# A two-block transformer kernel: the softmax-free attention's reciprocal moved from VectorE to ScalarE as Ln and Exp, and layernorm, transposes and loads issued earlier

## The chip, the cores and the metric

One core of one Trainium2 chip. The time is the device time of the kernel in microseconds; lower is better. Engines are called PE (TensorE), DVE (VectorE), ACT (ScalarE), POOL (GpSimd) and SP (which here only issues DMA). L165 is line 165 of the kernel that the profile belongs to. psum is the memory to which PE writes its products; they share a few buffers there (four of them tagged "mm"), each in use until ACT or DVE has read it.

## The reference

Two block types alternate, A B A B, on a bf16 tensor of 2048 tokens by 1024 features. A is linear attention, B a bilinear gated MLP without activation.

```python
def _A_ref(x, wqkv, wo):            # 32 heads of 32
    q, k, v = split(x @ wqkv)
    phi = lambda t: jnp.where(t > 0, t + 1, jnp.exp(t)) + 1e-6
    pq, pk = phi(q), phi(k)
    kv  = einsum("bhsd,bhse->bhde", pk, v);  z = einsum("bhsd->bhd", pk)
    num = einsum("bhqd,bhde->bhqe", pq, kv)
    den = einsum("bhqd,bhd->bhq", pq, z)[..., None] + 1e-6
    return (num / den) @ wo
def _B_ref(x, w_gate, w_up, w_down):
    return ((x @ w_gate) * (x @ w_up)) @ w_down
x = x + _A_ref(_layernorm(x), ...);  x = x + _B_ref(_layernorm(x), ...)   # and both once more
```

## The kernel before

Tokens are handled in four groups of 512 (four tiles of 128). The order of instructions on each engine is chosen by a scheduler when the kernel is built (the *compiled order*); the program gives it priorities and data dependences. An A layer has two stages. The *projection stage* makes phi(q), phi(k), v and adds up the key-value sums. The *output stage* is what this study is about:

```python
def layer_A():
    with tc.tile_pool(name="pA", bufs=1) as pA:
        pqT = pA.tile([P, KD, S], BF16, tag="pqT")
        KVm = pA.tile([P, KD, 2, P], BF16, tag="KVm")
        with ...:                                  # projection stage
            # ... wqkv loaded, per group: ln_transpose x4, q, k, v, key-value products (cut)
        with tc.tile_pool(name="pA2", bufs=1) as p2, tc.tile_pool(name="wA2", bufs=2) as work:
            # ... wo loaded here (cut)
            for g in range(NG):                    # output stage
                oT = work.tile([P, KD, G], BF16, tag="oT")
                for c in range(KD):
                    nps = psum.tile([P, NB], F32, tag="mm", bufs=4)      # numerator
                    nc.tensor.matmul(out=nps[:], lhsT=KVm[:, c, 0, :], rhs=pqT[:, c, g * G:(g + 1) * G], ...)
                    dps = psum.tile([P, NB], F32, tag="mm", bufs=4)      # denominator
                    nc.tensor.matmul(out=dps[:], lhsT=KVm[:, c, 1, :], rhs=pqT[:, c, g * G:(g + 1) * G], ...)
                    den = work.tile([P, NB], F32, tag="den")
                    nc.scalar.activation(out=den[:], in_=dps[:], func=ACT.Identity, bias=eps6[:], scale=1.0)
                    nc.vector.reciprocal(out=den[:], in_=den[:])
                    nc.vector.tensor_tensor(out=oT[:, c, :], in0=nps[:], in1=den[:], op=ALU.mult)
                for tl in range(TPG):              # output projection, 64 products per group
                    # ... ps = oT @ wo ; X += ps on DVE (cut)
```

`ln_transpose` (bn_stats, Sqrt on ACT, normalise on DVE, eight transposes on PE, a copy on ACT) stands at the head of each group, in A and in B. In B the gate and up weights stream through two buffers each, and each group ends with 224 down products.

## Time and profile before

The median is 1940.78 us (6 runs, 1938.94 to 1944.26). I cut the timeline at four kinds of marks on PE: the first projection product, the last key-value product, the first gate product, the last down product.

| stretch | layer 1 and 2, us | layer 3 and 4, us |
|---|---|---|
| start to first projection product | 18.1 | 5.7 (from the last down product) |
| projection stage | 202.5 | 197.3 |
| output stage (to first gate product) | 165.0 | 164.8 |
| gated layer | 591.4 | 590.9 |
| end | | 3.6 |

The page of the kernel before: busy time by engine, then forty equal slices of the span, each digit a tenth of busy share; PEclk is the granted PE clock in tenths.

```profile
PE 1765.8 (91%) x8320; PEld 805.7 (42%) x8320; DVE 889.6 (46%) x1287; ACT 359.7 (19%) x567; POOL 166.6 (9%) x138
...
PE   7999666799999999999999995677999999999999
...
DVE  8877899931131131121277769999211111111111
...
PEclk9999877899999999999999997788999999999999
```

PE is busy 91% of the span, and at full clock nearly everywhere; the two dips (slices 5 to 8 and 25 to 28, PE at 5 to 7, PEclk at 7 to 8) are the two output stages, and there DVE stands at 9. The table of stretches for just these two gives, per engine, busy microseconds and the number of instructions (POOL last), then PEclk:

```profile
core 0: us, PE busy (x) PEld busy (x) DVE busy (x) ACT busy (x) POOL busy (x), PEclk, DMA share, GB/s
220.60:385.60 165.00, 101.78 (x360) 38.18 (x361) 160.05 (x153) 28.97 (x44) 0.00 (x0) 0.74 0.13 40
1179.90:1344.70 164.80, 100.46 (x361) 37.74 (x361) 159.98 (x153) 28.97 (x44) 0.00 (x0) 0.76 0.13 40
```

DVE is busy 160 of 165 us. PE counts 101 us of work, but the 320 products of the stage (256 projections, 64 numerators and denominators) would take 69 us at the spacing seen where PE is never interrupted (224 down products in 48.35 us, 0.216 us each). So the stage is DVE bound, and PE work in it also runs slowly. The groups by line, with count, then busy us and mean ns of one, then the idle time before them and its releaser (what ended the wait), name the culprit:

```profile
L165 DVE RECIPROCAL den<-den 128x512 f32<-128x512 f32 x64 | 211.3, 3327 | 3.4 <-ACT den L164 3.4
...
L164 ACT ACTIVATE den<-dps,eps 128x512 f32<-128x512 f32 x64 | 43.7, 686 | 242.9 <-DVE oT L166 207.8 <-PE dps L161 18.2 <-DVE KVm L147 16.8
...
L74 ACT ACT_TABLE_LOAD x12 | 15.4, 1283 | 10.0 <-DMA X<-in_A_x_dram 9.8
L87 ACT ACT_TABLE_LOAD x11 | 14.1, 1283 | 0.2
```

One reciprocal of 128x512 takes 3327 ns, nearly five times any other DVE pass over that shape here (at most 0.69 us). ACT_TABLE_LOAD, 1283 ns each, is the instruction that the build puts on ACT before a function of another set. The timeline (start, duration, engine, line, what, and in brackets the idle time before it with its releaser) shows how it holds PE:

```profile
231.87 1.22 DVE L166 TENSOR_TENSOR oT<-nps,den 128x512 bf16<-128x512 f32 x2
232.55 0.59 PE L158 MATMUL nps<-pqT,KVm 128*128 128x512 bf16 x1 [5.98 <-DVE oT L166]
...
232.59 0.69 ACT L164 ACTIVATE den<-dps,eps 128x512 f32<-128x512 f32 x1 [6.66 <-DVE oT L166]
...
233.31 6.56 DVE L165 RECIPROCAL den<-den 128x512 f32<-128x512 f32 x2 [0.22 <-ACT den L164]
...
240.48 0.59 PE L158 MATMUL nps<-pqT,KVm 128*128 128x512 bf16 x1 [3.50 <-DVE oT L166]
```

Two reciprocals (6.56 us), two products, and only then a psum buffer for the next numerator: PE waits 5.98 us. The matmul after that wait takes 0.59 us instead of 0.38, and after the next such waits products follow 0.43 us apart instead of 0.216: PE restarted at a lower clock. The totals of the waits of PE say the same (us in total, times, longest); the third line is the transposes, which wait for ACT to empty a psum buffer:

```profile
PE nps L158 <- DVE oT L166: 63.0, 12, 6.0
PE ps L172 <- DVE oT L166: 35.0, 8, 4.5
...
PE pt L81 <- ACT xnT L82: 9.2, 17, 0.7
```

### The profile page before, as it was taken

What the parts mean: (1) busy time and instruction counts of PE and PEld (TensorE: products, weight loads), DVE (VectorE), ACT (ScalarE), POOL (GpSimd) and SP (SyncE); (2) the same over time, 40 slices, a digit from 0 to 9 for tenths busy, and PEclk for the clock granted to TensorE, in tenths of its full rate; (3) what the DMA queues carried; (4) which work ended last, traced back from release to release, by engine and by line L of the source; (5) the groups of instructions that cost most, each with busy time, mean ns of one, the idle gap of its engine ahead of it and who ended that gap; (6) DMA issues with size and microseconds to landing.
All of it is one profiled execution on the core that took longest, in us unless ns stands there. A gap on an engine that the chain in (4) does not pass through costs nothing.

```text
span 1939.3 us, 19949 instructions
## 1 busy us (share of the span) xinstructions
PE 1765.8 (91%) x8320; PEld 805.7 (42%) x8320; DVE 889.6 (46%) x1287; ACT 359.7 (19%) x567; POOL 166.6 (9%) x138
## 2 busy tenths in 40 slices
PE   7999666799999999999999995677999999999999
PEld 3444322344444444444444442223444444444444
DVE  8877899931131131121277769999211111111111
ACT  4332111111021021021043321112211111110110
POOL 3344100000000000000034341000000000000000
PEclk9999877899999999999999997788999999999999
DMA  6000400074044134124040004002740440450420
GB/s 217 1 1 1 130 0 0 20 263 145 29 128 133 44 106 155 44 87 130 1 131 1 1 1 130 0 0 81 243 132 22 151 153 22 131 173 23 130 87 22
DMA packets 145882, 158.57 MB, mean 82 GB/s; under 512 B 3456, under 2 KB 134528, under 8 KB 145792
## 3 DMA queue, kind: packets, MB, share of 16 engines
q1 hardware_dynamic: 135424, 138.42, 22.3%
q10 hardware_dynamic: 10368, 18.88, 2.8%
q8 instruction: 65, 1.06, 0.2%
q14 instruction: 25, 0.20, 0.0%
HBM read 153.09 MB, written 4.19 MB: 81 GB/s over the span
## 4 chain that ended last, share of the span: by engine, by line
PE 79%; DVE 13%; issue 3%; ACT 2%; DMA 1%; POOL 0%; ACTq 0%; DVEq 0%; POOLq 0%
PE ps L216 20%; PE gp L202 20%; PE up L206 20%; PE ps L124 11%; DVE den L165 8%; PE ps L114 5%; PE ps L172 3%; ACT xnT L82 2%; DVE oT L166 1%; DVE X L175 1%; PE kp L138 1%; DVE acc L143 1%; DMA wd<-in_B_w_down_dram 1%; DMA X<-in_A_x_dram 1%; DVE st L70 0%
## 5 line engine op out<-in xcount | busy, mean ns | idle before, releaser
L210 DVE TENSOR_TENSOR hT<-gs,up 128x512 bf16<-128x512 f32 x224 | 153.8, 687 | 599.7 <-PE up L206 575.9
L202 PE MATMUL gp<-xnT,wg 128*128 128x512 bf16 x1792 | 423.3, 379 | 4.6 <-ACT xnT L82 4.3
L206 PE MATMUL up<-xnT,wu 128*128 128x512 bf16 x1792 | 423.3, 379 | 0.0
L216 PE MATMUL ps<-wd,hT 128*128 128x512 bf16 x1792 | 388.1, 379 | 0.0
L202 PEld LDWEIGHTS <-wg 128*128 128x128 bf16 x1792 | 175.3, 98 | 215.3 <-issue 5.8
L206 PEld LDWEIGHTS <-wu 128*128 128x128 bf16 x1792 | 175.4, 98 | 211.4
L216 PEld LDWEIGHTS <-hT 128*128 128x128 bf16 x1792 | 175.4, 98 | 211.4
L209 ACT COPY gs<-gp 128x512 f32<-128x512 f32 x224 | 130.9, 585 | 626.2 <-PE gp L202 608.6
L124 PE MATMUL ps<-wqkv,xnT 128*128 128x512 bf16 x1024 | 234.0, 379 | 0.0
L165 DVE RECIPROCAL den<-den 128x512 f32<-128x512 f32 x64 | 211.3, 3327 | 3.4 <-ACT den L164 3.4
L172 PE MATMUL ps<-wo,oT 128*128 128x512 bf16 x512 | 152.3, 449 | 52.3 <-DVE oT L166 35.0
L219 DVE TENSOR_TENSOR X<-X,ps 128x512 bf16<-128x512 bf16 x64 | 44.0, 687 | 338.5 <-PE ps L216 338.5
L124 PEld LDWEIGHTS <-xnT 128*128 128x128 bf16 x1024 | 100.1, 98 | 105.5
L82 ACT COPY xnT<-pt 128x1024 bf16<-128x1024 bf16 x64 | 61.2, 1019 | 374.2 <-PE pt L81 374.1
L87 ACT ACTIVATE m<-m 128x512 f32<-128x512 f32 x128 | 80.1, 630 | 235.7 <-DVE m L86 235.5
L114 PE MATMUL ps<-xnT,wqkv 128*128 128x512 bf16 x512 | 119.4, 397 | 4.6 <-ACT xnT L82 4.1
L172 PEld LDWEIGHTS <-oT 128*128 128x128 bf16 x512 | 55.1, 109 | 151.5 <-issue 66.8
L86 DVE TENSOR_SCALAR m<-ps 128x512 f32<-128x512 f32 x128 | 88.1, 688 | 47.2 <-PE ps L114 34.3
L158 PE MATMUL nps<-pqT,KVm 128*128 128x512 bf16 x64 | 32.8, 512 | 70.6 <-DVE oT L166 63.0
L90 POOL TENSOR_TENSOR pk<-m,r 128x512 bf16<-128x512 f32 x64 | 81.0, 1267 | 130.4 <-ACT m L87 127.7
L90 POOL TENSOR_TENSOR pqT<-m,r 128x512 bf16<-128x512 f32 x64 | 81.1, 1272 | 119.9 <-ACT m L87 85.7
L164 ACT ACTIVATE den<-dps,eps 128x512 f32<-128x512 f32 x64 | 43.7, 686 | 242.9 <-DVE oT L166 207.8
(33 smaller groups left out, 727.8 us busy)
## 6 DMA issues: line engine op xcount, KB each, us to landing
wg<-in_B_w_gate_dram SPq DMA_DIRECT2D x56, 1024.0 KB, 5.4
wu<-in_B_w_up_dram SPq DMA_DIRECT2D x56, 1024.0 KB, 7.2
wd<-in_B_w_down_dram ACTq DMA_DIRECT2D x56, 256.0 KB, 4.7
wqkv<-in_A_wqkv_dram SPq DMA_DIRECT2D x12, 1024.0 KB, 11.8
wo<-in_A_wo_dram SPq DMA_DIRECT2D x4, 1024.0 KB, 9.4
X<-in_A_x_dram ACTq DMA_DIRECT2D x8, 256.0 KB, 5.8
X<-in_A_x_dram SPq DMA_DIRECT2D x8, 256.0 KB, 5.6
out_dram<-X SPq DMA_DIRECT2D x8, 256.0 KB, 2.0
```

Of the source, the lines that this page charges most:

```text
L82: nc.scalar.copy(out=xnT[:, :, col0:col0 + P], in_=pt[:])
L86: nc.vector.tensor_scalar_min(out=m[:], in0=ps, scalar1=0.0)
L90: nc.gpsimd.tensor_tensor(out=dst, in0=m[:], in1=r[:], op=ALU.add)
L114: nc.tensor.matmul(out=ps[:], lhsT=wqkv[:, k, c * P:(c + 1) * P], rhs=xnT[:, k, :], start=(k == 0), stop=(k == KD - 1))
L124: nc.tensor.matmul(out=ps[:], lhsT=xnT[:, k, tl * P:(tl + 1) * P], rhs=wqkv[:, k, D + n * NB:D + (n + 1) * NB], start=(k == 0), stop=(k == ...
L165: nc.vector.reciprocal(out=den[:], in_=den[:])
L172: nc.tensor.matmul(out=ps[:], lhsT=oT[:, c, tl * P:(tl + 1) * P], rhs=wo[:, c, n * NB:(n + 1) * NB], start=(c == 0), stop=(c == KD - 1))
L202: nc.tensor.matmul(out=gp[:], lhsT=wg[:, k, j * P:(j + 1) * P], rhs=xnT[:, k, :], start=(k == 0), stop=(k == KD - 1))
L206: nc.tensor.matmul(out=up[:], lhsT=wu[:, k, j * P:(j + 1) * P], rhs=xnT[:, k, :], start=(k == 0), stop=(k == KD - 1))
L209: nc.scalar.copy(out=gs[:], in_=gp[:])
L210: nc.vector.tensor_tensor(out=hT[:, f, :], in0=gs[:], in1=up[:], op=ALU.mult)
L216: nc.tensor.matmul(out=ps[:], lhsT=hT[:, f, tl * P:(tl + 1) * P], rhs=wd[:, f, n * NB:(n + 1) * NB], start=(f == 0), stop=(f == KF - 1))
```

## The change

The intent: take the reciprocal off DVE (1/d = exp(-ln d), on the nearly idle ACT), and take layernorm, transposes and loads off PE's path by issuing them before they are needed. The eight blocks c of 128 features of a group are now done in two halves of four. The core of the diff (shortened; "..." marks cuts):

```diff
-    for t in range(NT):
+    for t in range(TPG):                      # only group 0 of X before the weights
         eng.dma_start(out=X[:, t, :], in_=x_view[:, t, :])
...
+    def ln_stage(li, g):  ...                 # bn_stats, Sqrt, normalise of a group (xn: 4 buffers)
+    def tr_stage(li, g):  ...                 # its transposes and copies (xnT: 2 buffers)
+    def get_xnT(li, g):   ...                 # take it, or make it now
...                                            # projection stage
                     phi_from_psum(ps[:], pqT[:, c, g * G:(g + 1) * G], work)
+                ln_stage(li, g + 1)
                 for tl in range(TPG): ...
+                tr_stage(li, g + 1)
...                                            # output stage
-                for c in range(KD):
-                    nps = ...; dps = ...      # as above, with DVE reciprocal
+                if g == NG - 1:
+                    ln_stage(li + 1, 0)
+                for h in range(2):
+                    den = work.tile([P, KD // 2, NB], F32, tag="den")
+                    for cc in range(KD // 2):
+                        dps = psum.tile([P, NB], F32, tag="mm", bufs=4)
+                        nc.tensor.matmul(out=dps[:], lhsT=KVm[:, h * KD // 2 + cc, 1, :], rhs=pqT[...], ...)
+                        nc.scalar.activation(out=den[:, cc, :], in_=dps[:], func=ACT.Ln, bias=eps6[:], scale=1.0)
+                    nc.scalar.activation(out=den[:], in_=den[:], func=ACT.Exp, scale=-1.0)
+                    for cc in range(KD // 2):
+                        nps = psum.tile([P, NB], F32, tag="mm", bufs=4)
+                        nc.tensor.matmul(out=nps[:], lhsT=KVm[:, c, 0, :], rhs=pqT[...], ...)
+                        nc.vector.tensor_tensor(out=oT[:, c, :], in0=nps[:], in1=den[:, cc, :], op=ALU.mult)
...                                            # gated layer
-                tc.tile_pool(name="sB", bufs=2) as stream:
+                tc.tile_pool(name="sB", bufs=3) as stream:
+                ln_stage(next group or layer) before the down products, tr_stage after the second tile of them
+                if li == 3: store each tile of the output as soon as it is done
```

wo is also loaded during the projection stage instead of at the head of the output stage. The arithmetic is the same apart from the reciprocal.

More of the change, by code (lines that the diff above doesn't have):

```diff
@@ L57 @@
     x_view = A_x[0].rearrange("(t p) d -> p t d", p=P)
-    for t in range(NT):
+    for t in range(TPG):
         eng = nc.sync if t % 2 == 0 else nc.scalar
         eng.dma_start(out=X[:, t, :], in_=x_view[:, t, :])
+    xnp = ctx.enter_context(tc.tile_pool(name="xnp", bufs=2))
     FMAX = min(int(nc.vector.BN_STATS_FMAX), D)
@@ L65 @@
     NST = D // FMAX
-    def ln_transpose(t, xnT, col0, work):
-        st = small.tile([P, NST, 6], F32, tag="st")
-        for c in range(NST):
-            nc.vector.bn_stats(out=st[:, c, :], in_=X[:, t, c * FMAX:(c + 1) * FMAX])
-        mv = small.tile([P, 2], F32, tag="mv")
-        nc.vector.bn_aggr(out=mv[:], in_=st[:])
-        rstd = small.tile([P, 1], F32, tag="rstd")
-        nc.scalar.activation(out=rstd[:], in_=mv[:, 1:2], func=ACT.Sqrt, bias=eps5[:], scale=1.0)
-        nc.vector.reciprocal(out=rstd[:], in_=rstd[:])
-        xn = work.tile([P, D], BF16, tag="xn")
-        nc.vector.tensor_scalar(out=xn[:], in0=X[:, t, :], scalar1=mv[:, 0:1], scalar2=rstd[:],
-                                op0=ALU.subtract, op1=ALU.mult)
-        pt = psum.tile([P, KD, P], BF16, tag="tr")
-        for k in range(KD):
-            nc.tensor.transpose(out=pt[:, k, :], in_=xn[:, k * P:(k + 1) * P], identity=ident[:])
-        nc.scalar.copy(out=xnT[:, :, col0:col0 + P], in_=pt[:])
+    pending = {}
@@ new lines, with ln_stage @@
+    ready = {}
+    def ln_stage(li, g):
+        if li >= 4:
+            return
+        if g >= NG:
+            return
+        xns = []
+        for tl in range(TPG):
+            t = g * TPG + tl
+            st = small.tile([P, NST, 6], F32, tag="st")
+            for c in range(NST):
+                nc.vector.bn_stats(out=st[:, c, :], in_=X[:, t, c * FMAX:(c + 1) * FMAX])
+            mv = small.tile([P, 2], F32, tag="mv")
+            nc.vector.bn_aggr(out=mv[:], in_=st[:])
+            rstd = small.tile([P, 1], F32, tag="rstd")
+            nc.scalar.activation(out=rstd[:], in_=mv[:, 1:2], func=ACT.Sqrt, bias=eps5[:], scale=1.0)
+            nc.vector.reciprocal(out=rstd[:], in_=rstd[:])
+            xn = xnp.tile([P, D], BF16, tag="xn", bufs=4)
+            nc.vector.tensor_scalar(out=xn[:], in0=X[:, t, :], scalar1=mv[:, 0:1], scalar2=rstd[:],
+                                    op0=ALU.subtract, op1=ALU.mult)
+            xns.append(xn)
+        pending[(li, g)] = xns
@@ new lines, in tr_stage @@
+    def tr_stage(li, g):
+        if (li, g) not in pending:
+            return
+        xns = pending.pop((li, g))
+        xnT = xnp.tile([P, KD, G], BF16, tag="xnT")
+        for tl in range(TPG):
+            pt = psum.tile([P, KD, P], BF16, tag="tr")
+            for k in range(KD):
+                nc.tensor.transpose(out=pt[:, k, :], in_=xns[tl][:, k * P:(k + 1) * P], identity=ident[:])
+            nc.scalar.copy(out=xnT[:, :, tl * P:(tl + 1) * P], in_=pt[:])
+        ready[(li, g)] = xnT
@@ L84, in phi_from_psum, with get_xnT @@
+    def get_xnT(li, g):
+        if (li, g) not in ready:
+            ln_stage(li, g)
+            tr_stage(li, g)
+        return ready.pop((li, g))
     def phi_from_psum(ps, dst, work):
@@ L90, in phi_from_psum, with layer_A @@
         nc.gpsimd.tensor_tensor(out=dst, in0=m[:], in1=r[:], op=ALU.add)
-    def layer_A():
+    def layer_A(li):
         with tc.tile_pool(name="pA", bufs=1) as pA:
@@ L95, in layer_A @@
             KVm = pA.tile([P, KD, 2, P], BF16, tag="KVm")
+            wo = pA.tile([P, KD, D], BF16, tag="wo")
+            wov = A_wo.rearrange("(k p) n -> p k n", p=P)
             with tc.tile_pool(name="pA1", bufs=1) as p1, tc.tile_pool(name="wA1", bufs=2) as work:
@@ L100, in layer_A @@
                     nc.sync.dma_start(out=wqkv[:, :, n * NB:(n + 1) * NB], in_=wv[:, :, n * NB:(n + 1) * NB])
+                if li == 0:
+                    for t in range(TPG, NT):
+                        nc.sync.dma_start(out=X[:, t, :], in_=x_view[:, t, :])
                 acc = p1.tile([P, KD, 2 * P], F32, tag="acc")
@@ L106, in layer_A @@
                     nc.gpsimd.memset(vb[i][:, :, P:2 * P], 1.0)
+                for n in range(D // NB):
+                    nc.sync.dma_start(out=wo[:, :, n * NB:(n + 1) * NB], in_=wov[:, :, n * NB:(n + 1) * NB])
                 for g in range(NG):
-                    xnT = work.tile([P, KD, G], BF16, tag="xnT")
-                    for tl in range(TPG):
-                        ln_transpose(g * TPG + tl, xnT, tl * P, work)
+                    xnT = get_xnT(li, g)
                     for c in range(KD):
@@ L149, in layer_A @@
             with tc.tile_pool(name="pA2", bufs=1) as p2, tc.tile_pool(name="wA2", bufs=2) as work:
-                wo = p2.tile([P, KD, D], BF16, tag="wo")
-                wov = A_wo.rearrange("(k p) n -> p k n", p=P)
-                for n in range(D // NB):
-                    nc.sync.dma_start(out=wo[:, :, n * NB:(n + 1) * NB], in_=wov[:, :, n * NB:(n + 1) * NB])
                 for g in range(NG):
                     oT = work.tile([P, KD, G], BF16, tag="oT")
-                    for c in range(KD):
-                        nps = psum.tile([P, NB], F32, tag="mm", bufs=4)
-                        nc.tensor.matmul(out=nps[:], lhsT=KVm[:, c, 0, :], rhs=pqT[:, c, g * G:(g + 1) * G],
-                                         start=True, stop=True)
-                        dps = psum.tile([P, NB], F32, tag="mm", bufs=4)
-                        nc.tensor.matmul(out=dps[:], lhsT=KVm[:, c, 1, :], rhs=pqT[:, c, g * G:(g + 1) * G],
-                                         start=True, stop=True)
-                        den = work.tile([P, NB], F32, tag="den")
-                        nc.scalar.activation(out=den[:], in_=dps[:], func=ACT.Identity, bias=eps6[:], scale=1.0)
-                        nc.vector.reciprocal(out=den[:], in_=den[:])
-                        nc.vector.tensor_tensor(out=oT[:, c, :], in0=nps[:], in1=den[:], op=ALU.mult)
@@ new lines, in layer_A @@
+                    if g == NG - 1:
[4 more added lines that the diff above has]
+                            dps = psum.tile([P, NB], F32, tag="mm", bufs=4)
+                            nc.tensor.matmul(out=dps[:], lhsT=KVm[:, h * KD // 2 + cc, 1, :],
+                                             rhs=pqT[:, h * KD // 2 + cc, g * G:(g + 1) * G], start=True, stop=True)
+                            nc.scalar.activation(out=den[:, cc, :], in_=dps[:], func=ACT.Ln, bias=eps6[:], scale=1.0)
+                        nc.scalar.activation(out=den[:], in_=den[:], func=ACT.Exp, scale=-1.0)
+                        for cc in range(KD // 2):
+                            c = h * KD // 2 + cc
+                            nps = psum.tile([P, NB], F32, tag="mm", bufs=4)
+                            nc.tensor.matmul(out=nps[:], lhsT=KVm[:, c, 0, :], rhs=pqT[:, c, g * G:(g + 1) * G],
+                                             start=True, stop=True)
+                            nc.vector.tensor_tensor(out=oT[:, c, :], in0=nps[:], in1=den[:, cc, :], op=ALU.mult)
@@ L176, in layer_A, with layer_B @@
                                                     in1=ps[:], op=ALU.add)
-    def layer_B():
+                        if g == NG - 1 and tl == 1:
+                            tr_stage(li + 1, 0)
+    def layer_B(li):
         with tc.tile_pool(name="pB", bufs=1) as pB, tc.tile_pool(name="wB", bufs=2) as work, \
-                tc.tile_pool(name="sB", bufs=2) as stream:
+                tc.tile_pool(name="sB", bufs=3) as stream:
             wd = pB.tile([P, KF, D], BF16, tag="wd")
@@ L186, in layer_B @@
             for g in range(NG):
-                xnT = work.tile([P, KD, G], BF16, tag="xnT")
-                for tl in range(TPG):
-                    ln_transpose(g * TPG + tl, xnT, tl * P, work)
+                xnT = get_xnT(li, g)
                 for fb in range(FB):
@@ L210, in layer_B @@
                         nc.vector.tensor_tensor(out=hT[:, f, :], in0=gs[:], in1=up[:], op=ALU.mult)
+                if g + 1 < NG:
+                    ln_stage(li, g + 1)
+                else:
+                    ln_stage(li + 1, 0)
                 for tl in range(TPG):
@@ L220, in layer_B @@
                                                 in1=ps[:], op=ALU.add)
-    layer_A()
-    layer_B()
-    layer_A()
-    layer_B()
+                    if li == 3:
+                        nc.sync.dma_start(out=o_view[:, t, :], in_=X[:, t, :])
+                    if tl == 1:
+                        if g + 1 < NG:
+                            tr_stage(li, g + 1)
+                        else:
+                            tr_stage(li + 1, 0)
     o_view = out[0].rearrange("(t p) d -> p t d", p=P)
-    for t in range(NT):
-        eng = nc.sync if t % 2 == 0 else nc.scalar
-        eng.dma_start(out=o_view[:, t, :], in_=X[:, t, :])
+    layer_A(0)
+    layer_B(1)
+    layer_A(2)
+    layer_B(3)
 _INS = ['A_x', 'A_wqkv', 'A_wo', 'B_x', 'B_w_gate', 'B_w_up', 'B_w_down']
```

## The prediction

> **What bounds it now.** TensorE, unevenly. By the table of stretches, the two gated layers run PE 97 to 100% busy at clock 1.00. The attention-output stage (numerator, denominator, output projection; 222 to 385 us and 1182 to 1344 us) has PE busy 16 to 24 us of each 37, clock 0.56 to 0.82, and DVE nearly full. The chain of waits puts 7.6% of the span on the DVE reciprocal (3327 ns, 64 of them, 211 us). Full-rate matmuls are 0.216 us apart (224 in 48.35 us), so its 320 matmuls need 69 of about 164 us (last key-value product 220.6, first gate matmul 385.6). Other losses, from the timeline: first projection matmul at 18.1 us; 5.6 us at each group boundary of the projection stage (115.5 to 121.05), then 64 matmuls in 15.6 instead of 14.0 us; 3.5 us at each gated-layer boundary (531.06 to 534.60).
>
> **What changes.**
> 1. Reciprocal becomes Ln and Exp on ACT. DVE loses 211 us. Per half group ACT gains four Ln (0.69 us, like the present pass), one 128x2048 Exp (estimate 1.9 us, from 585 ns for 512 and 1019 ns for 1024 elements), and table loads. The Trainium skill (ScalarE: Activation LUTs, section Table sets) says one set holds both functions, but the compiled order shows a load before each: 65 loads against 23, about 23 per stage with the Sqrts mixed in. The trace shows 1283 ns each, the next activation following within 0.03 us, without the drain that page adds.
> 2. Normalisation and transposes move earlier. In the compiled order the gated layers' transposes lie inside the down products, but 72 transposes per stage land in the attention-output stage, with their Sqrts; most projection-stage boundaries still have them bunched, and 48 stand before the third layer.
> 3. Only four X tiles precede the weights; wo loads early; outputs leave as they finish (the last still at the end).
>
> **The new output stage** stays a latency chain: four denominators, four Ln, load, Exp, four numerators, four products, and only then free psum buffers for the next denominators; PE has numerators ahead of ready projection work, so it stands through the Exp. By hand, from trace durations, after the last key-value product: first Exp done at 7, second 15, third 23, group 0 done 36, group 1 61, group 2 101, all 126 us. This includes half-rate matmuls after gaps of 4 to 5 us, as the present trace shows (48 in 12.36 instead of 10.4 us at 370 us; the skill's TensorE: Matmul & The Clock Gate, Part 1, has the clock drop after about 3.4 us idle). So 164 becomes about 126: 38 saved per layer.
>
> **Sum.** Output stages 2 x 38 = 76; gated boundaries 2 x 6 = 12; projection stage 5 in the first and 9 in the third layer; start 3; about 105 to 110. 1941 - 110 = about 1831 us, range 1800 to 1862. Faster by over 2%: 0.95; within 2%: 0.04; slower: 0.01.
>
> **What would show it.** Output stage 115 to 137 us with ACT the releaser of PE (numerators waiting for den), clock below 0.9, ACT over 75 us busy in it, DVE total about 680 us. No gap beyond 0.5 us between down products and gate matmuls. Projection stage 190 to 200 us in the first layer, 188 to 197 in the third. First projection matmul at 14 to 16 us.
>
> **What would make it wrong.** If the Ln/Exp chains overlap the projection better than the order suggests, the stage falls to 100 us and the time under 1790. If X tiles queued behind the weights hold DVE, Sqrt loads delay the projection stage's Exps, or DVE adds stuck behind reciprocals waiting for Sqrt stall psum, up to 30 us come back.

## The result, and the profile after

The changed kernel takes 1812.40 us (median of 8 runs, 1810.91 to 1816.84) against 1942.63 us for the kernel before in the same rounds (16 runs): ratio 0.9335, 95% interval 0.9325 to 0.9345. Ratios here are the mean time of one kernel's fast runs over that of the other's fast runs of the same rounds, so not quite the ratio of the medians quoted.

| stretch, us | before | after | saved | predicted saving |
|---|---|---|---|---|
| start to first projection product | 18.1 | 14.7 | 3.4 | 3 |
| projection stage, layer 1 | 202.5 | 194.8 | 7.7 | 5 |
| output stage, layer 1 | 165.0 | 118.0 | 47.0 | 38 |
| gated layer 2 | 591.4 | 586.8 | 4.6 | 6 |
| boundary to layer 3 | 5.7 | 5.1 | 0.6 | 0 |
| projection stage, layer 3 | 197.3 | 187.0 | 10.3 | 9 |
| output stage, layer 3 | 164.8 | 115.5 | 49.3 | 38 |
| gated layer 4 and end | 594.6 | 587.4 | 7.2 | 6 |
| sum | 1939.3 | 1809.3 | 130.0 | 105 to 110 |

(Both columns are of the profiled executions. "Predicted saving" splits the terms of the sum.) The same views as before. The page:

```profile
PE 1727.5 (95%) x8320; PEld 799.2 (44%) x8320; DVE 694.2 (38%) x1223; ACT 443.3 (25%) x625; POOL 166.7 (9%) x138
...
PE   7999887999999999999999997789999999999999
...
DVE  7977675312211211211267776662111211211111
...
PEclk9999888999999999999999998999999999999999
```

The dips are narrower and shallower, DVE in them fell from 9 to between 5 and 7, and ACT took over 84 us of busy time (443.3 against 359.7). The table of stretches for the two output stages:

```profile
209.45:327.40 117.95, 89.81 (x392) 37.85 (x393) 73.21 (x155) 76.83 (x86) 0.00 (x0) 0.84 0.17 54
1106.40:1221.90 115.50, 87.43 (x393) 37.58 (x394) 73.23 (x155) 76.58 (x86) 0.00 (x0) 0.87 0.17 55
```

DVE went from 160 to 73 us, ACT from 29 to 77 us, and neither fills the 118 us; PEclk rose from 0.74 to 0.84. The groups by line of the new work:

```profile
L194 ACT ACTIVATE den<-dps,eps 128x512 f32<-128x512 f32 x64 | 40.6, 686 | 8.0 <-PE dps L192 7.4
L201 DVE TENSOR_TENSOR oT<-nps,den 128x512 bf16<-128x512 f32 x64 | 40.0, 682 | 63.3 <-ACT den L195 63.3
...
L195 ACT ACTIVATE den<-den 128x2048 f32<-128x2048 f32 x16 | 30.6, 1909 | 0.2
L85 ACT ACT_TABLE_LOAD x23 | 29.5, 1283 | 2.0 <-PEq L287 1.6
...
L194 ACT ACT_TABLE_LOAD x16 | 20.5, 1283 | 17.1 <-DVE KVm L181 16.8
L195 ACT ACT_TABLE_LOAD x16 | 20.5, 1283 | 0.3
```

For 512 denominators per partition Ln costs 686 ns (exactly what the Identity pass cost before) and Exp 1909 / 4 = 477 ns, together 1.16 us against 3.33 us; but Ln and Exp each bring a table load with every half group, 16 and 16, and L85's 23 are those of the layernorm's Sqrt. The timeline of the stage's first part:

```profile
213.51 1.28 ACT L194 ACT_TABLE_LOAD   x1 [8.40 <-DVE KVm L181]
...
214.81 2.42 ACT L194 ACTIVATE den<-dps,eps 128x512 f32<-128x512 f32 x4
215.54 2.32 PE L199 MATMUL nps<-pqT,KVm 128*128 128x512 bf16 x4 [3.06 <-ACT den L194]
...
218.54 1.91 ACT L195 ACTIVATE den<-den 128x2048 f32<-128x2048 f32 x1
...
220.48 2.48 DVE L201 TENSOR_TENSOR oT<-nps,den 128x512 bf16<-128x512 f32 x4 [7.04 <-ACT den L195]
221.22 0.58 PE L192 MATMUL dps<-pqT,KVm 128*128 128x512 bf16 x1 [3.36 <-DVE oT L201]
...
233.91 5.34 PE L207 MATMUL ps<-wo,oT 128*128 128x512 bf16 x24
...
235.60 1.91 ACT L195 ACTIVATE den<-den 128x2048 f32<-128x2048 f32 x1
```

Three things are to be seen. The numerators (L199, 215.54) start while the Exp has not begun: what they waited for is a psum buffer, which the Ln of a denominator frees. The next denominator (L192, 221.22) waits 3.36 us for a product: all four "mm" buffers hold numerators until the Exp is done. And 24 projection products (233.91) run while a later half's Exp (235.60) is still to come. The waits of PE:

```profile
PE ps L207 <- DVE oT L201: 27.6, 9, 4.3
PE dps L192 <- DVE oT L201: 13.4, 4, 3.4
...
PE nps L199 <- ACT den L194: 6.7, 4, 3.3
```

What PE now waits for in this stage is the DVE product oT, which in turn waits for the Exp; the transposes' waits at gated boundaries are gone (waits for xnT before a gate product: 4.3 us before, none after).

### The profile page after: what moved, and what is told of

Read it like the earlier page. It is cut to its first block, busy times and chain, and to the rows that moved or that the text cites. A ratio compares the mean times of both kernels' runs of the same rounds, so it can differ in the third digit from the quotient of the medians.

```text
span 1809.3 us, 19843 instructions
## 1 busy us (share of the span) xinstructions
PE 1727.5 (95%) x8320; PEld 799.2 (44%) x8320; DVE 694.2 (38%) x1223; ACT 443.3 (25%) x625; POOL 166.7 (9%) x138
## 5 line engine op out<-in xcount | busy, mean ns | idle before, releaser
L207 PE MATMUL ps<-wo,oT 128*128 128x512 bf16 x512 | 137.5, 415 | 31.3 <-DVE oT L201 27.6
L146 PE MATMUL ps<-xnT,wqkv 128*128 128x512 bf16 x512 | 113.4, 382 | 4.4 <-ACT xnT L102 4.1
L81 DVE BATCH_NORM_STATS2 st<-X 128x6 f32<-128x512 bf16 x128 | 85.8, 681 | 4.0 <-DMA X<-in_A_x_dram 2.6
L116 DVE TENSOR_SCALAR r<-ps 128x512 f32<-128x512 f32 x128 | 87.0, 680 | 0.0
L146 PEld LDWEIGHTS <-wqkv 128*128 128x128 bf16 x512 | 50.4, 99 | 64.6 <-issue 6.8
```

The costliest lines, as they stand in the source:

```text
L81: nc.vector.bn_stats(out=st[:, c, :], in_=X[:, t, c * FMAX:(c + 1) * FMAX])
L116: nc.vector.tensor_scalar(out=r[:], in0=ps, scalar1=0.0, scalar2=1e-6, op0=ALU.max, op1=ALU.add)
L146: nc.tensor.matmul(out=ps[:], lhsT=wqkv[:, k, c * P:(c + 1) * P], rhs=xnT[:, k, :], start=(k == 0), stop=(k == KD - 1))
L207: nc.tensor.matmul(out=ps[:], lhsT=oT[:, c, tl * P:(tl + 1) * P], rhs=wo[:, c, n * NB:(n + 1) * NB], start=(c == 0), stop=(c == KD - 1))
```

## The experiments

Twelve kernels were run; all gave correct results. "Stage" is the output stage of layers 1 and 3, from the last key-value product to the first gate product, or, where the scheduler moved gate products into the stage, to the last output projection (number of gate products inside in brackets, 0.216 us each).

| run | median us | ratio to before | stage us | table loads |
|---|---|---|---|---|
| changed kernel | 1812.40 | 0.9335 | 118.0, 115.5 | 65 |
| e1_lnexp_only | 1843.55 | 0.9501 | 120.9, 120.5 (6) | 69 |
| e2_hoist_only | 1899.98 | 0.9788 | 166.3, 164.8 (29) | 21 |
| e3_joint_table | 1795.04 | 0.9245 | 108.4, 104.5 | 45 |
| e4_one_table_all | 1758.13 | 0.9057 | 88.8, 89.1 (6) | 1 |
| e5_den_ahead | 1818.18 | 0.9351 | 103.8, 103.8 | 61 |
| e6_den_ahead_one_table | 1778.36 | 0.9149 | 83.3, 82.7 | 1 |
| e7_x_first | 1814.57 | 0.9334 | 116.1, 114.7 | 63 |
| e8_no_gated_hoist | 1820.57 | 0.9371 | 118.3, 116.2 | 65 |
| e9_den_ahead_two_bufs | 1790.76 | 0.9226 | 106.2, 106.5 (9) | 61 |
| e10_den_ahead_one_table_two_bufs | 1748.33 | 0.9009 | 85.6, 85.4 (8) | 1 |
| e11_third_den_buffer | 1845.87 | 0.9501 | 115.9, 118.6 | 65 |
| e12_den_outside | 1741.18 | 0.8969 | 80.9, 80.9 (8) | 1 |

(For e5, e6 and e11 the stage is taken to its last output projection; the first gate product came 7 us later, as told below.)

### Which half of the change makes the gain: e1 and e2

My theory: the reciprocal leaving DVE. The rival: the earlier normalisation and transposes. e1 takes only the Ln and Exp loop into the kernel before; e2 puts the old loop back into the changed kernel.

```diff
 # e1, in the kernel before          # e2, in the changed kernel: the reverse
-                for c in range(KD):      # numerator, denominator, Identity, reciprocal, product
+                for h in range(2):       # four denominators, Ln; one Exp; four numerators, products
```

> The kernel before, with only the inner loop of the attention-output stage taken from the change (Ln and Exp on ACT, halves of four); no hoisting. Theory (the reciprocal leaving DVE makes most of the gain): that stage falls from 165 to 105-115 us per layer, the time to about 1941 - 2 x 55 = 1830 us (1815 to 1845). Rival (the early normalisation and transposes make the gain): stage stays above 150 us, time 1915 or more.

> The changed kernel, with the reciprocal loop of before put back; all hoisting, DMA order and buffers kept. Theory: only the start, the projection stages and the gated boundaries gain (together 33 us in the two traces), and the attention-output stage stays DVE bound, now with about 20 us of hoisted normalisation per layer on the same DVE: stage 160 to 180 us, time 1905 to 1935 us. Rival (hoisting is the gain): 1860 us or less.

Measured: e1 0.9501, so 97 us of 1942 saved; e2 0.9788, 41 us saved (its interval, 0.9773 to 0.9802, reaches over the 2% mark, so the verdict at 2% is unclear; it lies clear of no change). Both parts are real and the reciprocal is the larger; the rival falls. e1's time lay at the edge of its expectation and its stage (121 us, 6 gate products inside) a little above it: the trace showed that the scheduler had moved transposes and Sqrts into the shortened stage by itself (69 table loads), so e1 is not the change without any hoisting. e2 was 5 us faster than expected: its DVE-bound stage kept its length while 29 gate products slipped into PE's idle time there. The two savings add to 138 us, the change saves 129: 9 us overlap. The moved gate products (29 of 0.216 us, 6 us per layer) are a candidate for that, but no run isolates it.

### What the table loads cost: e3 and e4

The Trainium skill, ScalarE: Activation LUTs, section Table sets, says that one shipped set holds both exp and ln. The compiled order of the changed kernel nevertheless has a load before each, because the pass that places them when the kernel is built chose two different sets. In e3 it was told that only the joint set has them; in e4 the layernorm also uses Ln and Exp.

```diff
+    def _tables(*a, **k):                     # e3, e4: at build time only
+        t = {n: set(v) for n, v in _orig(*a, **k).items()}
+        for n in t:
+            if n != "natural_log_exp_and_others":
+                t[n] -= {_AF.Exp, _AF.Ln}
+        return t
+    _hs.get_activation_tables = _tables
 # e4 besides
-            nc.scalar.activation(out=rstd[:], in_=mv[:, 1:2], func=ACT.Sqrt, bias=eps5[:], scale=1.0)
-            nc.vector.reciprocal(out=rstd[:], in_=rstd[:])
+            nc.scalar.activation(out=rstd[:], in_=mv[:, 1:2], func=ACT.Ln, bias=eps5[:], scale=1.0)
+            nc.scalar.activation(out=rstd[:], in_=rstd[:], func=ACT.Exp, scale=-0.5)
```

> The changed kernel, with the pass that places table loads told that only the joint set holds Ln and Exp: 45 loads instead of 65, arithmetic unchanged. If the chain (denominators, Ln, load, Exp, product) bounds the stage, only the load between Ln and Exp is on it, 8 x 1.28 = 10 us per layer, the load before Ln being hidden while PE waits for products: stage about 107 us, time about 1792 us (1785 to 1800). If ACT's total work bounds the stage, all 20 loads count: about 1.28 x 10 = 13 us per layer too, 1786. If neither matters (transposes or the PE clock bound it), 1805 to 1812.

> As the joint-table run, and the layernorm's Sqrt and DVE reciprocal replaced by Ln and Exp(-0.5 x): one table load in the whole kernel. The Sqrt loads sit in the chain of groups 1 and 3 and in the second half of group 2, about four per layer: 5 us per layer below the joint-table run; elsewhere nothing (projection stages are PE and DVE bound). Stage about 102 us, time about 1780 us (1770 to 1792). If the hoisted Sqrts cost nothing on the chain, equal to the joint-table run within 3 us.

e3 came as expected (1795, stage 10 us shorter): ratio 0.9245, 17 us below the changed kernel. It does not separate a chain from ACT's sum of work, for both had predicted nearly the same here. It is the clean price of loads alone, since ACT's instructions in the stage stand in the same order as in the changed kernel, and PE's too as far as they are on record. e4 saved 37 us more, where I had expected some 12. The tables of stretches, output stage of layer 1, e3 and then e4 (columns as before):

```profile
209.70:318.00 108.30, 85.57 (x384) 37.18 (x393) 73.12 (x155) 63.88 (x76) 0.00 (x0) 0.87 0.18 59
```

```profile
209.80:298.60 88.80, 78.54 (x373) 35.14 (x380) 69.60 (x136) 46.26 (x74) 0.00 (x0) 0.94 0.23 72
```

ACT lost 17.6 us, and the groups by line list 13 table loads in this stage of e3 and none in e4: 13 x 1.283 = 16.7 us. My expectation had counted four loads on the chain; with Ln and Exp in one set, each visit of a Sqrt costs a load in and a load out. But e4 changed more than the loads: its compiled order is another. The two kernels have the same order of products on PE and keep step until 239 us; then e3 stands before its next long run of projection products and e4 does not (PE, e3 first, then e4):

```profile
248.41 4.19 PE L207 MATMUL ps<-wo,oT 128*128 128x512 bf16 x9 [4.26 <-DVE oT L201]
```

```profile
248.55 10.52 PE L207 MATMUL ps<-wo,oT 128*128 128x512 bf16 x47
```

In e3 such a run of 47 or 48 projection products goes on beside an Exp in two of the four groups, as in the changed kernel; in e4 in three, and the fourth starts without such a stand. So the 37 us are the price of loads and order together; no run separates them, and that every load delayed a denominator is not shown. In e4 PE idles 10 us instead of 23 (stretch less PE busy), and its busy time falls by 7 us for nearly the same work (20 transposes fewer, 6 gate products more), because PEclk rises from 0.87 to 0.94. The hoisted layernorms were cheap in work (a Sqrt of 128x1 takes 0.29 us) and dear in table loads.

### Is it a chain: e5, e6, e9 to e12

The timeline said: product, free psum buffer, denominator, Ln, load, Exp, product. To break that ring without taking any wait away, I issued each half's denominators one half ahead.

```diff
+                den_stage(0)                       # four denominators, Ln, one Exp of half s
                 for g in range(NG):
                     for h in range(2):
+                        den_stage(2 * g + h + 1)   # before the numerators of half 2g+h
+                        den = dens.pop(2 * g + h)
...                                                 # den: tag with bufs=3 (e5, e6)
```

> The changed kernel with the denominators of the next half (four products, Ln, Exp) issued one half ahead of the numerators, three den buffers instead of two; table loads stay (61). Theory: what is left in the attention-output stage is the serial chain product - free psum - denominator - Ln - load - Exp - product, so taking the denominators out of it leaves the larger of ACT's 77 us and TensorE's 73 us plus fill: stage 90 to 100 us instead of 118, time about 1770 us (1760 to 1785). Rival (ACT's work with its table loads bounds the stage whatever the order): stage stays above 110 us, time above 1800.

> The one-table kernel with the denominators one half ahead. There the chain has already lost its loads (stage 89 us, of which about 3 us are gate products that the scheduler moved in, TensorE at full rate 73 us). Theory of the chain: most of the rest goes, stage 80 us, time about 1742 us (1734 to 1750). Rival (the rest is startup, mask products and boundaries): within 5 us of the one-table kernel, 1753 or more.

By time both failed: 1818 and 1778 us, no clear difference from the changed kernel (0.9351 against 0.9335, the intervals overlap) and 18 us more than e4. But the stage itself had become 12 to 14 us shorter in e5 (103.8) and 4 to 5 us shorter in e6 than in e4 (less its 6 gate products). The waits of PE in e5:

```profile
PE gp L248 <- DMA wg<-in_B_w_gate_dram: 15.0, 2, 7.6
PE nps L210 <- ACT den L195: 12.0, 6, 4.6
...
PE up L252 <- DMA wu<-in_B_w_up_dram: 9.2, 2, 4.7
```

A new wait for gate weights had appeared. When were they asked for? The timeline of SP, changed kernel first, then e5, and PE's first gate product in e5:

```profile
213.60 0.37 SPq L227 DMA_DIRECT2D wg<-in_B_w_gate_dram  x1
```

```profile
314.56 0.37 SPq L238 DMA_DIRECT2D wg<-in_B_w_gate_dram  x1
```

```profile
321.79 3.57 PE L248 MATMUL gp<-xnT,wg 128*128 128x512 bf16 x8 [7.38 <-DMA wg<-in_B_w_gate_dram]
```

In the changed kernel the first gate weights are issued at the start of the output stage, in e5 only after its last projection, 101 us later; PE stands 7.4 us for them, and again afterwards. From the tile shapes, the pools of the output stage take 52 KB (pqT, KVm, wo) plus oT 16 KB plus den 16 KB = 84 KB per partition with two den buffers, and 92 KB with three; the gated layer's streamed weights begin behind wd, hT and gs, at 56 + 28 + 4 = 88 KB. With three buffers the den tiles overlie the first weight buffer, and the load must wait until the stage is over. (The addresses are worked out from the shapes; that the loads move is measured.) e9 and e10 use two buffers, which suffice; e11 is the control, the changed kernel with a third den buffer and nothing else.

```diff
-                    den = work.tile([P, KD // 2, NB], F32, tag="den", bufs=3)   # e9 from e5, e10 from e6
+                    den = work.tile([P, KD // 2, NB], F32, tag="den", bufs=2)
 # e11, in the changed kernel
-                        den = work.tile([P, KD // 2, NB], F32, tag="den")
+                        den = work.tile([P, KD // 2, NB], F32, tag="den", bufs=3)
```

> The den-ahead kernel with two den buffers in place of three. In the three-buffer run the stage itself took 104 us instead of 118 and 115.5, but the first gate weights were issued only at its end (314.6 us, against 213.6 in the changed kernel), and TensorE then waited 12 us per layer for weights. Theory: the third buffer (8 KB per partition) lies where the first streamed gate weights go; without it the loads issue at about 213 us again and only the gain of the stage is left: stage 102 to 106 us, no wait for weights, time about 1788 us (1780 to 1796). Rival (the reordering itself delays the weights): wait for weights stays, time above 1808.

> One table for all, denominators half a group ahead, two den buffers. From the three-buffer run: stage 83 us instead of 86 to 89, weights on time: time about 1750 us (1743 to 1756), the fastest so far; if the chain no longer matters once the loads are gone, equal to the one-table kernel, 1758 us.

> The changed kernel with nothing but a third den buffer. Theory of the displaced weights: order on every engine nearly unchanged in the attention-output stage, stage still 114 to 119 us, but gate weights issued at its end, about 15 us lost per layer in and after the switch (as in the den-ahead run: 7.5 us before the first gate product and 7.6 us inside the gated layer): time about 1840 us (1832 to 1848). Rival (an extra buffer is harmless or helps): 1812 us or less.

All three came as expected: 1790.76, 1748.33 and 1845.87 us. e9 is 21 us below the changed kernel (0.9226 against 0.9335), so the ring did cost about 11 us per layer (at most 2.6 us of it can be the two table loads fewer per stage). e11 is 32 us above it (0.9501), with the waits in the output stage unchanged and the waits for weights new:

```profile
PE gp L237 <- DMA wg<-in_B_w_gate_dram: 14.1, 2, 7.1
PE dps L192 <- DVE oT L201: 13.4, 4, 3.4
PE up L241 <- DMA wu<-in_B_w_up_dram: 9.1, 2, 4.6
```

What remained with the loads in place (e9, 106 us for work that needs 74: 69 us for the stage's products, 3 for its 59 transposes, at 0.45 us per eight, as they follow one another in the down products of the changed kernel, and 2 for the 9 gate products) is mostly the loads again: PE's largest wait there is for Ln on ACT (13.0 us over both layers), and e10, without loads in the stage and in nearly the same compiled order (50 transposes in it instead of 59), has a stage 21 us shorter.

e12 takes one more piece. In the changed kernel the first table load and Ln of a stage wait 8.40 us for the mask products KVm (the first line of the timeline after), although the first denominators are issued at 210.7. In the compiled order the first Ln of e10 carries waits for DVE and for DMA queues besides its own product on PE, which points to an earlier tile in the same place. e12 gives den a place of its own, and there the first Ln waits for PE alone:

```diff
-                    den = work.tile([P, KD // 2, NB], F32, tag="den", bufs=2)
+                    den = pA.tile([P, KD // 2, NB], F32, tag="den", bufs=2)
```

> As the two-buffer one-table den-ahead kernel, with the den buffers in the pool of the whole attention layer instead of that of the output stage, so that the first Ln no longer waits for all sixteen mask products whose source (the sums) its buffer overlies. In the changed kernel that wait let the first Ln start 4 us after its denominator was there (214.8 us, first denominator product at 210.7). Expect 2 to 4 us less per layer: time 4 to 8 us below the two-buffer kernel, about 1744 us. If the start of the stage is bound by the mask products anyway: within 2 us of it.

Measured 1741.18 us, 7 us below e10, as expected; the first Ln now waits for the denominator itself:

```profile
211.99 3.00 ACT L195 ACTIVATE den<-dps,eps 128x512 f32<-128x512 f32 x5 [6.00 <-PE dps L193]
```

It is the fastest version, 10.3% below the kernel before and 3.9% below the changed one (0.8969 / 0.9335). Two lines of its page:

```profile
PE 1705.2 (98%) x8320; PEld 795.2 (46%) x8320; DVE 688.0 (40%) x1159; ACT 366.9 (21%) x625; POOL 167.6 (10%) x138
...
PEclk9999999999999999999999999999999999999999
```

PE is busy 98% of the span, at 9 tenths of its clock or more in every slice.

### The small parts: e7 and e8

```diff
 # e7: all 16 X tiles first, on two queues, as before
-    for t in range(TPG):
+    for t in range(NT):
 # e8: in the gated layer, nothing early for its own next group
-                if g + 1 < NG: ln_stage(li, g + 1)
-                        if g + 1 < NG: tr_stage(li, g + 1)
```

> The changed kernel with all sixteen X tiles loaded first, on two queues, as before. Theory: only the start moves, first projection matmul at 17 to 18.5 instead of 14.7 us, the time 3 us longer (2 to 4): 1815 us. Rival (X tiles queued behind the weights hold DVE in the first projection stage): equal or shorter time than the changed kernel.

> The changed kernel without the early normalisation and transposes inside the gated layers (the calls for the next group taken out; those into the next attention layer stay). Theory: 32 transposes stand again at two boundaries per gated layer where the scheduler cannot move them (the first boundary is served from the attention stage), each costing 1.7 us beyond the transposes' own 1.8: time 6 to 12 us longer, 1818 to 1824 us. Rival (the scheduler moved them anyway, or three weight buffers made the gain): within 2 us of the changed kernel.

e7 is inconclusive by time: 0.9334 against 0.9335, an interval of 0.002 each way. Its trace shows the start as expected, first projection product at 17.39 us instead of 14.68, and the projection stage ending 2.8 us later; in this profiled execution the output stages were 1 to 2 us shorter, so the small loss is not visible in the sum. The rival, X tiles that hold DVE, finds no support: the projection stage was 194.8 us in both. e8 is 7 us slower (0.9371), inside the expectation: at its boundaries the transposes stand again between down and gate products (618.5 to 622.1 us), while in the changed kernel they lie inside the down products.

## Why the prediction was right, and where its size was off

- **What bounds it, and which part pays.** Right. DVE's reciprocal bound the output stages; e1 and e2 show 97 and 41 us for the two parts.
- **Table loads.** Right in number (65, each 1283 ns, next activation at once) and in that they lie on the path (e3; e9 against e10). What I underestimated in e4's expectation, loads and order together, is not a term of the prediction's sum.
- **Start, projection stages, gated layers.** Right within 3 us each: 3.4, 7.7 and 10.3, 4.6 and 7.2 us saved against 3, 5 and 9, 6 and 6. Layer 3's projection stage ended at 187.0 us, just under the 188 to 197 I had named.
- **"Output stages 2 x 38 = 76": the mis-sized term.** It measured 47.0 + 49.3 = 96.3 us, which is the whole difference between 1831 and 1812. The step behind it was "PE has numerators ahead of ready projection work, so it stands through the Exp". The numerators do not read the Exp; they need only psum buffers, which Ln frees. So where numerators of the next half stood ahead of 48 projection products, PE ran both while the load and the Exp were under way, and ran the 48 at full rate (two times 24 in 5.3 us), not at the half rate of the prediction's example (48 in 12.36 us). In layer 1 the step held for six of the eight halves, where PE stood 2.3 to 4.3 us for oT (20.8 us in all), and failed for two, whose Exps ran beside the 48 projection products of groups 0 and 2. Two such stands less are about 7 us (an estimate from the mean of the six), of the 8 us by which the stage came in under 126. It is, in part, the overlap that the prediction had named under "What would make it wrong".

How the hand-made chain compares, in us after the last key-value product of layer 1:

| mark | predicted | measured |
|---|---|---|
| first Exp done | 7 | 11.0 |
| second | 15 | 19.0 |
| third | 23 | 28.1 |
| group 0 projected | 36 | 35.4 |
| group 1 | 61 | 60.0 |
| group 2 | 101 | 93.5 |
| all | 126 | 118.0 |

The first Exp was 4 us later than predicted, because the first load waited for the mask products (removed in e12), and the stage still ended 8 us earlier: one error hid the other in groups 0 and 1, and that these came within 1 us of the prediction is luck. That "numerators waiting for den" would be the visible releaser was wrong too; they wait only 6.7 us in all, and for Ln. The waits are those of denominators and projections for oT (13.4 and 27.6 us).
- **Half-rate matmuls.** Right in kind. The Trainium skill, TensorE: Matmul & The Clock Gate, Part 1, has the clock fall after about 3.4 us idle; here gaps of 3.36 us were followed by products 0.43 us apart. But that is no sharp limit in this trace: a gap of 2.26 us (before 229.24 us) was followed by products 0.43 us apart too, and one of 2.92 us (before 1182.26 us) by products 0.216 us apart. PEclk in the stage was 0.84 and 0.87, under the 0.9 predicted. In the changed kernel PE idles 28 us of the 118 and works 90 where 73 us would do at full rate.

## What to carry to other kernels

A slow operation moved to an idle engine becomes a latency, so look next at who holds buffers while waiting for it: here the psum buffers of numerators and the order of issue were worth 11 us per layer, and the ACT table loads about 21 (e9 against e10). Count table loads in the compiled order, both ways of each visit, before moving transcendental work into a stage, because a 0.3 us Sqrt can cost 2.6 us of loads; and compare the compiled orders before giving a difference to the edit alone, as e3 and e4 show. Ask of every added buffer what it overlies: one of 8 KB per partition delayed the next layer's weights by more than 100 us and cost 32 us in all.

## What the Trainium skill lacked or had wrong

- ScalarE: Activation LUTs, What ACT_TABLE_LOAD costs: the 1283 ns agree with the trace; the drain of about 1380 ns that the page adds to every switch is not seen here (load at 213.51 for 1.28 us, next activation at 214.81; and the load at 217.24 starts 0.02 us after the Ln before it).
- ScalarE: Activation LUTs, Table sets: it says that ln then exp needs one load because a joint set exists. Here the build gave each its own load (16 and 16, 65 in all) until it was told to use the joint set (45), and one set for everything needed the Sqrt replaced (1 load, 1758 us against 1795, in another compiled order).
- The same page, What it computes, sends Reciprocal to VectorE, and no page gives its time: 3327 ns for 128x512 f32, against 1163 ns of ACT for Ln and its share of Exp (686 + 1909 / 4).
- No page tells that a tile's place on chip ties a later layer's prefetch to an earlier stage: the third 8 KB buffer moved the first gate load from 213.6 to 326.7 us and cost 32 us (e11).
